# Attention denominators as one run of column-tiled products, other places for the M products, and another order of the first loads

## The chip, the cores and the metric

The kernel runs on one core of a Trainium2 chip. The metric is the device time of one execution in microseconds (us). Executions of one kernel agree within about 0.2%; all runs here are in the fast state (granted TensorE clock 0.997 to 1.0). The experiments ran in several rounds on several chips, each beside the kernel before, whose median moved from 739.8 to 740.2 us between them: differences of some tenths of a us between kernels of different rounds are not resolved by the medians alone.

Engine names in the profile: PE is TensorE's matmuls, PEld its weight loads, DVE is VectorE, ACT is ScalarE, POOL is GpSimd, SP issues the DMAs.

## The reference, cut to what matters

```python
xn = layernorm(x)                                   # x: 2048 x 1024
q, k, v = heads(xn @ wqkv)                          # 32 heads of 32
phi = lambda t: where(t > 0, t + 1, exp(t)) + 1e-6
kv  = einsum("bhsd,bhse->bhde", phi(k), v);  z = phi(k).sum(s)
den = einsum("bhqd,bhd->bhq", phi(q), z) + 1e-6
s   = (phi(q) @ kv / den) @ wo
g   = silu((silu(x_ @ w_gate) * (x_ @ w_up)) @ w_down)   # x_ = xn
out = x + s * g
```

## The kernel before

The kernel works in two passes over 1024 rows each. Within a pass the big products (q, gate, up, then down and the attention output) are split by Strassen's scheme into seven products each, so PSUM banks are scarce: a bank has to be drained by ScalarE or VectorE before TensorE may start the next product in it. `M` is the product of the summed `kv` and `wo`, made of 16 small products in pass 0.

The program is not written in its final order. Every operation is recorded, and a scheduler in Python then runs a simple simulation with a planned duration per operation, and fixes from it the order in which each engine's queue holds its instructions. On the chip each queue is worked off in that order: in the traces of the changed kernel and of a_twice (below), which share a plan, all 1395 VectorE instructions come in the same order although their waits differ. So an instruction that has to wait holds up all that stand behind it.

```python
def mm_cost(mms):                                   # TensorE, us
    return sum(max(r.shape[-1] / 2400.0 + 0.0026, 0.03) for (_, _, r, _, _) in mms)
def act(reads, writes, o, i, func, src="ps", **kw): # ScalarE
    return PL.op("act", reads, writes, lambda h: h.activation(o, i, func, **kw),
                 nel(o) / 1200.0 + (0.055 if src == "ps" else 0.095))
def dve(reads, writes, fn, n, rate=0.96):           # VectorE
    return PL.op("dve", reads, writes, fn, n / (rate * 1000.0) + 0.07)
...                                                 # in Plan.schedule, for every engine but TensorE:
    rdy = [o for o in a if o.ready <= t]
    o = min(rdy, key=lambda o: (o.dl, o.idx)) if rdy else min(a, key=lambda o: (o.ready, o.dl))
    ...
    free[e] = s + o.busy
    o.done = s + o.busy + o.lat
```

The denominators: after each evicted tile of phi(q), a pair of products with 32 output columns each is put off by seven steps; all pairs of a pass collect in one bank. `recip` then evicts, inverts and stores them, and `normalise_part` scales phi(q) later.

```python
def den_mm():
    if p not in den:
        den[p] = (balloc_part(), set())
    db, seen = den[p]
    mms = []
    for q in (2 * j, 2 * j + 1):
        mms.append((ps[db][32 * q:32 * q + 32, 0:256], Zh[:, g, :],
                    o[:, (q % 2) * 256:(q % 2) * 256 + 256], q not in seen, False))
        seen.add(q)
    pe_mm([named("Zh", g), zh_r, orr], [bank_r[db]], mms)
defer(7, den_mm)
```

Of the kernel before, what the change touches and what calls it, by code (L numbers as in the profile page):

```python
# [9 lines left out]
ACT = mybir.ActivationFunctionType  # L10
ALU = mybir.AluOpType
# [6 lines left out]

class Op:
    __slots__ = ("eng", "fn", "busy", "lat", "nbytes", "sem", "preds", "succs", "idx", "dl", "start", "done",  # L20
                 "ev", "pecum", "npred", "ready", "urgent")


class Region:
# [6 lines left out]
class Plan:  # L31
# [14 lines left out]
    def op(self, eng, reads, writes, fn, busy, sem=None, nbytes=0, urgent=0.0, cow=None, after=None):  # L46


        o = Op()
        o.eng, o.fn, o.busy, o.sem, o.nbytes, o.urgent = eng, fn, busy, sem, nbytes, urgent  # L50
        o.lat = 0.0 if sem is not None else self.LAT[eng]
        o.idx = len(self.ops)
        preds = set()
        for r in reads:
            for k in r.keys:
                preds.update(self.lastw.get(k, ()))
        if cow is not None:
            preds.update(cow.preds)
        if after is not None:
            preds.add(after)  # L60
        for r in writes:
            for k in r.keys:
                if cow is None:
                    preds.update(self.lastw.get(k, ()))
                    preds.update(self.readers.get(k, ()))
        for r in reads:
            for k in r.keys:
                self.readers.setdefault(k, []).append(o)
        for r in writes:
            for k in r.keys:  # L70
                if cow is None:
                    self.lastw[k] = [o]
                    self.readers[k] = []
                else:
                    self.lastw[k].append(o)
        o.preds = preds
        o.succs = []
        for p in preds:
            p.succs.append(o)
        o.pecum = self.pecum  # L80
        if eng == "pe":
            self.pecum += busy
            self.lastpe = o
        self.ops.append(o)
        return o

    def schedule(self):
        ops = self.ops
        for o in reversed(ops):
            d = o.pecum if o.eng == "pe" else o.pecum + 30.0  # L90
            for s in o.succs:
                extra = (4.0 + o.nbytes / 200e3) if o.sem is not None else o.busy + o.lat
                d = min(d, s.dl - extra)
            o.dl = d - o.urgent
        pes = [o for o in ops if o.eng == "pe"]
        cum = [o.pecum + o.busy for o in pes]
        for o in ops:
            if o.sem is not None and o.succs:
                k = bisect_right(cum, o.dl - self.lead) - 1
                if k >= 0 and pes[k] not in o.preds:  # L100
                    o.preds.add(pes[k])
                    pes[k].succs.append(o)
        for o in ops:
            o.npred = len(o.preds)
            o.ready = 0.0
        free = {e: 0.0 for e in self.ENGS}
        dma_free = 0.0
        avail = {e: [] for e in self.ENGS}
        pe_next = deque(o for o in ops if o.eng == "pe")
        for o in ops:  # L110
            if o.npred == 0:
                avail[o.eng].append(o)
        order = []
        done = set()
        total = len(ops)
        while len(order) < total:
            best = None
            for e in self.ENGS:
                a = avail[e]
                if not a:  # L120
                    continue
                t = free[e]
                if e == "pe":
                    lim = None
                    n = 0
                    for o in pe_next:
                        if n >= self.window:
                            lim = o.idx
                            break
                        n += 1  # L130
                    cand = [o for o in a if lim is None or o.idx < lim]
                    if not cand:
                        continue
                    rdy = [o for o in cand if o.ready <= t + 0.05]
                    o = min(rdy, key=lambda o: o.idx) if rdy else min(cand, key=lambda o: (o.ready, o.idx))
                else:
                    rdy = [o for o in a if o.ready <= t]
                    o = min(rdy, key=lambda o: (o.dl, o.idx)) if rdy else min(a, key=lambda o: (o.ready, o.dl))
                s = max(t, o.ready)
                if best is None or s < best[0]:  # L140
                    best = (s, e, o)
            s, e, o = best
            o.start = s
            if o.sem is not None:
                free[e] = s + 0.08
                b = max(s + 1.0, dma_free)
                dma_free = b + o.nbytes / 230e3
                o.done = dma_free + 1.8
            else:
                free[e] = s + o.busy  # L150
                o.done = s + o.busy + o.lat
            avail[e].remove(o)
            if e == "pe":
                done.add(o)
                while pe_next and pe_next[0] in done:
                    pe_next.popleft()
            order.append(o)
            for q in o.succs:
                q.npred -= 1
                q.ready = max(q.ready, o.done)  # L160
                if q.npred == 0:
                    avail[q.eng].append(q)
        self.order = order
        return order
# [55 lines left out]
def build_kernel(nc, A_x, A_wqkv, A_wo, B_w_gate, B_w_up, B_w_down, out, WINDOW=6, NWARM=14, NPE=4, LEAD=12.0):  # L220
# [12 lines left out]
    with ExitStack() as es:  # L233
# [20 lines left out]
        def named(*key):  # L254
            return Region([key])
# [30 lines left out]
        banks = deque(range(8))  # L286
        bare = deque()
        is_bare = set()

        def balloc(fresh=False):  # L290

            if fresh and bare:
                b = bare.popleft()
                is_bare.discard(b)
                return b
            return banks.popleft()
# [5 lines left out]
            return b  # L302

        def bfree(b):
            (bare if b in is_bare else banks).append(b)

        def sem(name):
# [350 lines left out]
        def t_tile(i):  # L658
# [10 lines left out]
            for q, halves in enumerate(((0, 4), (4, 4)) if i == 0 else ((0, 8),)):  # L669
# [3 lines left out]
                pe_tr([s.r, ident_r], [bank_r[b]],  # L673
                      [(pb[:, k, :], xa[:, (k0 + k) * 128:(k0 + k + 1) * 128], ident[:, :]) for k in range(n)])
                xr = xt_r(i, k0, n)
                if q == 0:
                    act([bank_r[b]], [xr], dst[:, k0:k0 + n], pb, ACT.Identity)
                else:
                    dve([bank_r[b]], [xr], lambda h, k0=k0, n=n, pb=pb: h.tensor_copy(dst[:, k0:k0 + n], pb), n * 128)
# [113 lines left out]
                st.direct = direct  # L793
            return st

        for n, (fn, args) in enumerate(((x_load, (0,)), (wkv_load, (0, 1, 0)), (x_load, (1,)), (wkv_load, (0, 1, 1)),
                                        (wkv_load, (0, 0, 0)), (wkv_load, (0, 0, 1)), (x_load, (2,)),
                                        (wkv_load, (1, 1, 0)), (wkv_load, (1, 1, 1)), (x_load, (3,)),
                                        (wkv_load, (1, 0, 0)), (wkv_load, (1, 0, 1)))):
# [211 lines left out]
        def q_load(p, s):  # L1011
            return wload(wqkv_v[:, :, s * 512:(s + 1) * 512], QJ[p][s])

        den = {}
        PQ0 = 52 * KB

        def pq_tile(g, j):
# [3 lines left out]
        def q_pair(p, s, stats, at, go=True):  # L1021
            stat, jstat = stats

            def evac(w):
                def f(i, j, ap, r, bank):
                    g = 2 * (2 * s + w) + i
                    o, orr = pq_tile(g, j)
                    phi_evac(ap, r, o, orr, "ps" if bank is not None else "sb")

                    def den_mm():  # L1030
                        if p not in den:
                            den[p] = (balloc_part(), set())
                        db, seen = den[p]
                        mms = []
                        for q in (2 * j, 2 * j + 1):
                            mms.append((ps[db][32 * q:32 * q + 32, 0:256], Zh[:, g, :],
                                        o[:, (q % 2) * 256:(q % 2) * 256 + 256], q not in seen, False))
                            seen.add(q)
                        pe_mm([named("Zh", g), zh_r, orr], [bank_r[db]], mms)
                    defer(7, den_mm)  # L1040
                return f
            s0, s1 = (xset(stat, w, XV[p], evac(w), d_ring) for w in range(2))
            pair = Pair(s0, s1, joint_of(jstat, s0, s1) if QJ[p][s] else None, at)
# [3 lines left out]

        def recip(p):

            flush()  # L1050
            db = den[p][0]
            e = rr_ring.take()
            ea, ra, rb = e.ap(F32, 0, KB), e.ap(F32, KB, KB), e.ap(BF16, 0, KB // 2)
            er, rr = e.sub(0, KB).r, e.sub(KB, KB).r
            dve([bank_r[db]], [er], lambda h: h.tensor_scalar(ea, ps[db][:, 0:256], 16.0, EPS_PHI, ALU.mult, ALU.add), 256)
            bfree(db)
            for q in range(4):
                dve([er], [e.sub(KB + q * 256, 256).r], lambda h, q=q: h.reciprocal(
# [290 lines left out]
        for p in range(2):  # L1349
            for k, n in order:  # L1350
# [2 lines left out]
                if (p, k, n) == (0, "q", 0):  # L1353
                    at = {"5_1": [kv_done], "3_0": [kvt]}
                if p == 0 and (k, n) in (("g", 0), ("q", 1), ("u", 0)):
                    at = {w: [build_m] for w in ("2_1 6_1 7_1 3_1 4_1" + " 2_0" * (k == "u")).split()}
                if (k, n) == ("u", 0):
                    at["7_0"] = at.get("7_0", []) + [partial(recip, p)]
                if n == 1 and k in "gu":
                    at = {w: [partial(normalise_part, p, "gu".index(k), h)] for h, w in enumerate(("2_1", "7_1"))}  # L1360
                if last_pair[0] is not None and (p, k, n) == (1, "q", 0):
                    pass
                elif k == "q":
# [81 lines left out]
```

## Time and profile before

739.85 us, the median of 3 runs (739.5 to 740.21). The profiled execution spans 739.1 us.

| what | number | view |
|---|---|---|
| TensorE busy | 722.5 us | page, part 1 |
| share of the chain of work that ended last: PE, ACT, DVE | 86%, 7%, 4% | page, part 4 |
| start to start of 512- and 256-column matmuls | 216 and 109 ns | timeline |
| time that 2790, 868 and the small ones need at that rate | about 707 us | worked out |
| TensorE's late starts from 125 to 715 us | 7.1 us | timeline, summed |

The two lines of the page that this rests on: busy time by engine, and the chain that ended last, by engine.

```profile
PE 722.5 (98%) x3878; PEld 365.9 (50%) x3894; DVE 599.3 (81%) x1398; ACT 396.6 (54%) x740; POOL 16.2 (2%) x35
PE 86%; ACT 7%; DVE 4%; DMA 1%; issue 1%; SPq 0%; POOL 0%; ACTq 0%
```

TensorE bounds the kernel. As matmuls overlap (a 512-column one is shown 379 ns long, and the next starts 216 ns after it), "busy" hides short losses, so I read starts: the next lines are the timeline of TensorE (start us, us, engine, line, operation, out<-in, form, count, and in brackets idle time and what ended it).

```profile
133.48 0.38 PE L209 MATMUL ps<-W 128*128 128x256 f16 x2
133.70 0.38 PE L209 MATMUL ps<-X,W 128*128 128x256 f16 x2
134.01 0.29 PE L209 MATMUL ps<-H,Zh 128*32 128x256 bf16 x2
134.23 0.39 PE L209 MATMUL ps<-W 128*128 128x256 f16 x2
134.46 0.81 PE L209 MATMUL ps<-X,W 128*128 128x512 f16 x3
...
474.33 0.38 PE L209 MATMUL ps<-TM,X 128*128 128x256 f16 x2
474.64 0.52 PE L209 MATMUL ps<-H,Zh 128*32 128x256 bf16 x8
475.48 0.61 PE L209 MATMUL ps<-X 128*128 128x512 f16 x2 [0.32 <-DVE ps L344]
```

Two 256-column products take 0.22 us from start to start (133.48 to 133.70). Before the denominator pair (`H,Zh`, 128*32) it is 0.31 (133.70 to 134.01) and after it another 0.22. A lone pair thus costs 0.31 us: 93 ns to get in, and 216 ns until the next product starts. At 474.64, four pairs that happen to stand together take 0.23 us from first to last start.

Where TensorE waits for others: these lines of its timeline have the longest brackets between 200 and 715 us, in the normalisation of pass 0 and in the q stage of pass 1.

```profile
211.22 0.39 PE L209 MATMUL ps<-X,W 128*128 128x256 f16 x2 [0.35 <-ACT ps L337]
223.66 0.39 PE L209 MATMUL ps<-X,W 128*128 128x256 f16 x2 [0.50 <-ACT ps L337]
...
441.23 0.39 PE L209 MATMUL ps<-P,W 128*128 128x256 f16 x2 [0.93 <-DVE H L707]
...
449.17 0.60 PE L209 MATMUL ps<-P,W 128*128 128x512 f16 x2 [1.03 <-ACT ps L337]
```

And the table by stretches (length, then busy us and count of PE, PEld, DVE, ACT, POOL, the clock, DMA share and GB/s). VectorE works 110.5 of 114 us in this stretch of pass 1.

```profile
core 0: us, PE busy (x) PEld busy (x) DVE busy (x) ACT busy (x) POOL busy (x), PEclk, DMA share, GB/s
436.00:550.00 114.00, 111.35 (x651) 60.17 (x650) 110.47 (x280) 80.43 (x160) 0.00 (x0) 1.00 0.40 127
```

### The profile page before, as it was taken

How to read it: one execution, taken by the hardware profiler on the slowest of the kernel's cores; microseconds unless marked ns; L12 is line 12 of the kernel's file. 1: busy time of each engine (PE TensorE's matmuls, PEld its weight loads, DVE VectorE, ACT ScalarE, POOL GpSimd, SP SyncE). 2: the span in 40 equal slices, each digit the busy share in tenths (PEclk: the TensorE clock that was granted, in tenths of full speed). 3: DMA queues.
4: the chain of work that ended last, by engine and by line, in shares of the span. 5: the costliest groups of instructions: out<-in, count | busy, mean ns of one | idle time of the engine just before them, and what ended most of it. 6: DMA issues, size and time to landing. Idle time of an engine off the chain costs nothing.

```text
span 739.1 us, 10502 instructions
## 1 busy us (share of the span) xinstructions
PE 722.5 (98%) x3878; PEld 365.9 (50%) x3894; DVE 599.3 (81%) x1398; ACT 396.6 (54%) x740; POOL 16.2 (2%) x35
## 2 busy tenths in 40 slices
PE   7999999999999999999999999999999999999996
PEld 3444444454555555544444444455555555444442
DVE  6989868989899988886466879999998988757353
ACT  2776554787696565623232266577866655223231
POOL 2201100000000000000000000000000000000000
PEclk9999999999999999999999999999999999999999
DMA  9363235124573323371846434217525245374822
GB/s 302 96 114 72 44 109 175 59 79 158 162 243 104 115 62 110 100 232 40 198 113 167 150 106 111 97 62 229 182 103 172 72 136 152 90 164 109 184 65 50
DMA packets 135219, 94.00 MB, mean 127 GB/s; under 512 B 32512, under 2 KB 131072, under 8 KB 135168
## 3 DMA queue, kind: packets, MB, share of 16 engines
q1 hardware_dynamic: 135168, 93.34, 44.5%
q8 instruction: 30, 0.49, 0.3%
q14 instruction: 21, 0.17, 0.1%
HBM read 75.50 MB, written 10.62 MB: 117 GB/s over the span
## 4 chain that ended last, share of the span: by engine, by line
PE 86%; ACT 7%; DVE 4%; DMA 1%; issue 1%; SPq 0%; POOL 0%; ACTq 0%
PE ps L209 86%; ACT TM L337 3%; ACT H L337 3%; DMA W<-in_A_x_dram 1%; ACT L337 1%; DVE H L707 1%; DVE W L344 1%; ACT ps L337 1%; DVE TM L706 0%; ACT W L337 0%; DVE H L344 0%; PE ps L216 0%; DVE TM L344 0%; DVE stats L637 0%; ACT X L337 0%
## 5 line engine op out<-in xcount | busy, mean ns | idle before, releaser
L209 PE MATMUL ps<-X,W 128*128 128x512 f16 (+1 forms) x1408 | 312.9, 361 | 1.1 <-ACT ps L337 0.9
L337 ACT ACTIVATE TM<-ps 128x512 f16<-128x512 f32 (+2 forms) x337 | 182.0, 557 | 156.6 <-PE ps L209 154.0
L209 PE MATMUL ps<-H,W 128*128 128x512 f16 (+1 forms) x891 | 206.1, 379 | 0.9 <-DVE TM L707 0.4
L209 PEld LDWEIGHTS ps<-X,W 128*128 128x128 f16 (+1 forms) x1408 | 136.1, 98 | 120.5 <-ACT ps L337 1.4
L344 DVE TENSOR_TENSOR W<-W 128x256 f16<-128x256 f16 (+6 forms) x424 | 170.0, 440 | 7.8 <-DMA W<-in_B_w_down_dram 5.7
L344 DVE TENSOR_TENSOR ps<-ps,TM 128x256 f32<-128x256 f32 (+1 forms) x218 | 117.5, 540 | 34.1 <-PE ps L209 33.1
L209 PEld LDWEIGHTS ps<-H,W 128*128 128x128 f16 (+1 forms) x896 | 87.1, 98 | 104.2 <-DVE TM L707 0.9
L337 ACT ACTIVATE H<-ps 128x512 f16<-128x512 f32 (+1 forms) x126 | 75.3, 602 | 64.6 <-PE ps L209 64.4
L337 ACT ACTIVATE ps<-ps 128x512 f32<-128x512 f32 (+1 forms) x156 | 78.7, 505 | 57.6 <-PE ps L209 52.6
L209 PE MATMUL ps<-P,W 128*128 128x256 f16 (+1 forms) x440 | 90.0, 323 | 2.1 <-ACT ps L337 1.0
L209 PE MATMUL ps<-W 128*128 128x256 f16 (+1 forms) x328 | 70.3, 299 | 0.5 <-DVE W L344 0.3
L344 DVE TENSOR_TENSOR TM<-ps,TM 128x512 f32<-128x512 f32 (+1 forms) x60 | 40.9, 682 | 31.2 <-PE ps L209 30.9
L337 ACT ACTIVATE TM<-TM 128x512 f16<-128x512 f32 (+1 forms) x61 | 38.0, 622 | 48.9 <-DVE TM L344 47.4
L209 PEld LDWEIGHTS ps<-P,W 128*128 128x128 f16 (+1 forms) x440 | 42.5, 98 | 34.1 <-ACT ps L337 1.7
L344 DVE TENSOR_TENSOR H<-H,TM 128x512 f16<-128x512 f16 x112 | 45.8, 417 | 12.9 <-ACT H L337 12.5
L344 DVE TENSOR_TENSOR H<-H 128x1024 f16<-128x1024 f16 (+2 forms) x82 | 50.3, 629 | 0.8 <-PE ps L209 0.3
L209 PEld LDWEIGHTS ps<-W 128*128 128x128 f16 (+1 forms) x328 | 30.9, 98 | 27.1 <-DVE W L344 2.7
L344 DVE TENSOR_TENSOR TM<-TM 128x512 f16<-128x512 f16 (+1 forms) x59 | 24.2, 419 | 18.6 <-DMA TM<-TM 11.0
L209 PE MATMUL ps<-H,X 128*128 128x512 bf16 (+1 forms) x133 | 32.5, 380 | 2.5 <-ACT X L337 0.7
L344 DVE TENSOR_TENSOR W<-H 128x1024 f16<-128x1024 f16 x40 | 26.9, 685 | 5.2 <-PE ps L209 4.9
L209 PE MATMUL ps<-TM,W 128*128 128x256 f16 (+1 forms) x144 | 30.9, 296 | 0.0
L706 DVE TENSOR_SCALAR TM<-TM 128x512 f16<-128x512 f16 x64 | 18.0, 286 | 10.6 <-ACT TM L337 10.5
(82 smaller groups left out, 419.4 us busy)
## 6 DMA issues: line engine op xcount, KB each, us to landing
W<-in_B_w_gate_dram SPq DMA_DIRECT2D x14, 1024.0 KB, 5.2
W<-in_B_w_up_dram SPq DMA_DIRECT2D x14, 1024.0 KB, 5.2
W<-in_B_w_down_dram SPq DMA_DIRECT2D x16, 896.0 KB, 6.2
W<-in_A_x_dram SPq DMA_DIRECT2D x16, 256.0 KB, 3.1
H<-in_A_wqkv_dram SPq DMA_DIRECT2D x8, 512.0 KB, 8.5
W<-in_A_wqkv_dram SPq DMA_DIRECT2D x4, 1024.0 KB, 5.3
H<-r_scratch SPq DMA_DIRECT2D x32, 128.0 KB, 3.8
q_scratch<-H SPq DMA_DIRECT2D x8, 512.0 KB, 3.1
```

The costliest lines, as they stand in the source:

```text
L209: last = h.matmul(o, l, r, start=st, stop=sp, skip_group_check=True)
L337: return PL.op("act", reads, writes, lambda h: h.activation(o, i, func, **kw), nel(o) / 1200.0 + (0.055 if src == "ps" else 0.095))
L344: return dve(reads, writes, lambda h: h.tensor_tensor(o, a, b, op), nel(o), 1.92 if fast else 0.96)
L706: dve([e.r], [b.r], lambda h: h.tensor_scalar(ba, ea, 1.0, EPS_PHI, ALU.min, ALU.add), 512, 2.6)
L707: dve([src_r, b.r], [out_r], lambda h: h.scalar_tensor_tensor(out_ap, src, 0.0, ba, ALU.max, ALU.add), 512)
```

## The change

Its intent: spend the change of tiling mode once a pass, not at each pair; hold no bank for the denominators during the q products; put the M products where banks are free; and load the first two tiles of x before the weights.

```diff
@@ balloc: which bank a fresh product gets
-            if fresh and bare:
+            if fresh and bare and (len(banks) < 3 or freed[bare[0]] < freed[banks[0]]):
@@ transposes of the first tile
-                if q == 0:
+                if q == 0 or i == 0:
                     act([bank_r[b]], [xr], dst[:, k0:k0 + n], pb, ACT.Identity)
@@ first loads
-        ... ((x_load, (0,)), (wkv_load, (0, 1, 0)), (x_load, (1,)), (wkv_load, (0, 1, 1)),
+        ... ((x_load, (0,)), (x_load, (1,)), (wkv_load, (0, 1, 0)), (wkv_load, (0, 1, 1)),
@@ den_mm is gone; recip
-            flush()
-            db = den[p][0]
+            db = balloc_part()
+            mms, rd = [], [zh_r]
+            for g in range(NG):
+                rd.append(named("Zh", g))
+                for q in range(4):
+                    o, orr = pq_tile(g, q // 2)
+                    rd.append(orr)
+                    mms.append((ps[db][32 * q:32 * q + 32, 0:256], Zh[:, g, :],
+                                o[:, (q % 2) * 256:(q % 2) * 256 + 256], g == 0, False))
+            pe_mm(rd, [bank_r[db]], mms)
...
-            dve([bank_r[db]], [er], lambda h: h.tensor_scalar(ea, ps[db][:, 0:256], 16.0, EPS_PHI, ...), 256)
+            act([bank_r[db], eps_r], [er], ea, ps[db][:, 0:256], ACT.Identity, bias=epsc[:, :], scale=16.0)
@@ where the steps stand (k: q, gate or up; n: block)
-                    at = {w: [build_m] for w in ("2_1 6_1 7_1 3_1 4_1" + " 2_0" * (k == "u")).split()}
-                if (k, n) == ("u", 0):
-                    at["7_0"] = at.get("7_0", []) + [partial(recip, p)]
-                if n == 1 and k in "gu":
-                    at = {w: [partial(normalise_part, p, "gu".index(k), h)] for h, w in enumerate(("2_1", "7_1"))}
+                    at = {"2_0": [build_m], "6_0": [build_m], "2_1": [build_m] * 2, "6_1": [build_m] * 2}
+                if (k, n) == ("g", 1):
+                    at = {"2_1": [partial(recip, p)]}
+                if (k, n) in (("u", 1), ("g", 2)):
+                    at = {w: [partial(normalise_part, p, "ug".index(k), h)] for h, w in enumerate(("2_1", "7_1"))}
```

Some lines of the change (a field `boost`, always 0) have no effect and are left out.

More of the change, by code (lines that the diff above doesn't have):

```diff
@@ L20 @@
     __slots__ = ("eng", "fn", "busy", "lat", "nbytes", "sem", "preds", "succs", "idx", "dl", "start", "done",
-                 "ev", "pecum", "npred", "ready", "urgent")
+                 "ev", "pecum", "npred", "ready", "urgent", "boost")
 class Region:
@@ L51, in op @@
         o.lat = 0.0 if sem is not None else self.LAT[eng]
+        o.boost = 0.0
         o.idx = len(self.ops)
@@ L137, in schedule @@
                     rdy = [o for o in a if o.ready <= t]
-                    o = min(rdy, key=lambda o: (o.dl, o.idx)) if rdy else min(a, key=lambda o: (o.ready, o.dl))
+                    o = min(rdy, key=lambda o: (o.dl - o.boost, o.idx)) if rdy else min(a, key=lambda o: (o.ready, o.dl))
                 s = max(t, o.ready)
@@ L288, in build_kernel @@
         is_bare = set()
+        freed = [0] * 8
         def balloc(fresh=False):
-            if fresh and bare:
+            if fresh and bare and (len(banks) < 3 or freed[bare[0]] < freed[banks[0]]):
                 b = bare.popleft()
@@ L304, in bfree @@
         def bfree(b):
+            freed[b] = len(PL.ops)
             (bare if b in is_bare else banks).append(b)
@@ L794, in kv_set @@
             return st
-        for n, (fn, args) in enumerate(((x_load, (0,)), (wkv_load, (0, 1, 0)), (x_load, (1,)), (wkv_load, (0, 1, 1)),
+        for n, (fn, args) in enumerate(((x_load, (0,)), (x_load, (1,)), (wkv_load, (0, 1, 0)), (wkv_load, (0, 1, 1)),
                                         (wkv_load, (0, 0, 0)), (wkv_load, (0, 0, 1)), (x_load, (2,)),
@@ L1012, in q_load @@
             return wload(wqkv_v[:, :, s * 512:(s + 1) * 512], QJ[p][s])
-        den = {}
         PQ0 = 52 * KB
@@ L1028, in f @@
                     phi_evac(ap, r, o, orr, "ps" if bank is not None else "sb")
-                    def den_mm():
-                        if p not in den:
-                            den[p] = (balloc_part(), set())
-                        db, seen = den[p]
-                        mms = []
-                        for q in (2 * j, 2 * j + 1):
-                            mms.append((ps[db][32 * q:32 * q + 32, 0:256], Zh[:, g, :],
-                                        o[:, (q % 2) * 256:(q % 2) * 256 + 256], q not in seen, False))
-                            seen.add(q)
-                        pe_mm([named("Zh", g), zh_r, orr], [bank_r[db]], mms)
-                    defer(7, den_mm)
                 return f
@@ L1054, in recip @@
             er, rr = e.sub(0, KB).r, e.sub(KB, KB).r
-            dve([bank_r[db]], [er], lambda h: h.tensor_scalar(ea, ps[db][:, 0:256], 16.0, EPS_PHI, ALU.mult, ALU.add), 256)
+            act([bank_r[db], eps_r], [er], ea, ps[db][:, 0:256], ACT.Identity, bias=epsc[:, :], scale=16.0)
             bfree(db)
```

## The prediction

> **What bounds the kernel now.** TensorE. The page has PE busy 722.5 of 739.1 us at full clock, and PE with 86% of the chain of work that ended last. In the timeline, 512-column matmuls start every 216 ns and 256-column ones every 109 ns; the program's 2790 and 868 of these, with the small ones, need about 707 us. The rest is start-up, tail, waits and the denominator products.
>
> **Denominators (the main term).** In the timeline each pair of 32-column products starts 309 ns after a 512-column matmul instead of 216 (93 ns, the length of their weight load), its two products start 3 ns apart, and what follows starts 216 ns later. So a lone pair costs 0.31 us of PE. Pass 0 has 16 lone pairs (5.0 us); pass 1 has 12 entries, some of several pairs (about 4 us). The trace already shows short runs: at 474.6 us four pairs follow each other at 115 and 106 ns, and four products start within 5 ns. This agrees with the Trainium skill, "TensorEngine Tiling (Array Packing)", Key Properties: a change of tiling mode drains the engine, different tiles run in parallel. A run of 32 is then 8 groups of four at 0.11 us plus one entry and one exit: an estimate of 1.1 us a pass. Saved: 9.0 - 2.2 = 6.8 us of PE work.
>
> **Waits around it.** Starts later than these rates allow, summed from the timeline: about 1.6 us at 139-163 us (M products waiting for a bank that ScalarE drains), 1.2 us at 211 and 224 us (ScalarE full: 9.5 of 10 and 11.9 of 12 us, normalisation), 2.9 us at 437, 441, 449 and 475 us. The den bank is no longer held through the q pairs and M products move to steps with more free banks; but the new order has four M products in a row, with one bank twice. I expect 1.2 us less in sum. The normalisation moves by one pair with the same ScalarE work, so its waits move rather than vanish.
>
> **What takes some back.** VectorE: the table by stretches has it busy 113 of 116 us from 436 to 550 us, and 39 of 40 from 200 to 240. With PE faster by 4 us in the first of these, VectorE ends some waits. I take off 1.5 us.
>
> **Start.** PE loses 5.2 us in the first 20 us. x tile 1 landed at 7.54 us and should now land near 4.3; but VectorE now does tile 1's statistics before it normalises tile 0, so the first real matmul should come about 1 us later (8.7 instead of 7.65), after which tile 1 no longer interrupts. The later wkv landings (9.1 to 19.4 us) stay, and VectorE is 98% busy from 20 to 40 us. I expect 1.0 us gained.
>
> **Sum.** -6.8 - 1.2 + 1.5 - 1.0 = -7.5 us: 732.3 us, range 729 to 736.5. Faster by over 2%: 0.02; within 2%: 0.97; slower: 0.01.
>
> **What would show it.** 32 products within about 1.0 us, two entries in all. PE's missing time in 128-180 us down by over 4 us, in 436-480 us by 3 to 5. First real matmul near 8.7 us; at 26 us PE about 1 us ahead. From 240 to 420 and 560 to 720 us the rhythm unchanged, only shifted.
>
> **What would make it wrong.** Weight loads of the run not hidden: 0.2 us per group of four, 0.8 us more a pass. VectorE saturated in pass 1, so nothing of that pass's 3 us arrives. M products in a row waiting for ScalarE. A slower start, as both halves of tile 0 now go through ScalarE. Better: all waits near 440-475 us gone, 3 us more.

## The result, and the profile after

735.4 us, the median of 4 runs (735.19 to 735.52), against 740.03 for the kernel before in the same rounds (739.5 to 740.36): 4.6 us less. Ratio 0.9938, 95% interval 0.9921 to 0.9955. Here and below, a ratio is the mean time of one kernel's fast runs over that of the other's of the same rounds, so not quite the ratio of the medians quoted. All outputs are right.

The same two lines of the page after the change:

```profile
PE 717.2 (98%) x3894; PEld 365.8 (50%) x3894; DVE 596.9 (81%) x1395; ACT 397.1 (54%) x743; POOL 14.1 (2%) x35
PE 80%; DVE 11%; ACT 7%; issue 1%; DMA 0%; POOL 0%; ACTq 0%; DVEq 0%
```

TensorE lost 5.3 us of busy time, but its share of the chain fell from 86 to 80%, and VectorE's rose from 4 to 11%. The timeline of TensorE around the run of pass 1 shows both the gain and a new loss:

```profile
478.31 1.03 PE L210 MATMUL ps<-P,W 128*128 128x512 f16 x4
479.26 1.06 PE L210 MATMUL ps<-H,Zh 128*32 128x256 bf16 x32
480.25 1.90 PE L210 MATMUL ps<-X,W 128*128 128x512 f16 x8
481.99 1.46 PE L210 MATMUL ps<-P,W 128*128 128x256 f16 x8
484.54 1.04 PE L210 MATMUL ps<-X,W 128*128 128x512 f16 x4 [1.09 <-DVE ps L347]
...
488.08 0.39 PE L210 MATMUL ps<-W 128*128 128x256 f16 x2 [0.77 <-DVE ps L347]
```

The 32 products take 1.06 us, and the run as a whole delays the next product by 1.08 us, in both passes. But 4 us later TensorE waits 1.09 us and then 0.77 us for VectorE to evict a bank (`ps`). The same stretch in the table shows VectorE as busy as before:

```profile
436.00:550.00 114.00, 110.40 (x664) 61.29 (x663) 110.31 (x283) 81.56 (x162) 0.00 (x0) 1.00 0.41 127
```

An account of the time from the end of the k and v stage (the last product into the `kv` banks) to the end of the program, from the starts of TensorE in the two traces: 617.7 us before, 613.3 after, 4.4 less. The denominators cost 9.1 us before and 2.2 after (-6.9). The late starts of all other products grew by 2.6 us. So the main term came as predicted, and more than a third of it came back as waits. The question of the experiments is why.

### The profile page after: what moved, and what is told of

Same layout as the page of the kernel before. It is cut to its first block, busy times and chain, and to the rows that moved or that the text cites. A ratio compares the mean times of both kernels' runs of the same rounds, so it can differ in the third digit from the quotient of the medians.

```text
span 733.8 us, 10527 instructions
## 1 busy us (share of the span) xinstructions
PE 717.2 (98%) x3894; PEld 365.8 (50%) x3894; DVE 596.9 (81%) x1395; ACT 397.1 (54%) x743; POOL 14.1 (2%) x35
## 4 chain that ended last, share of the span: by engine, by line
PE 80%; DVE 11%; ACT 7%; issue 1%; DMA 0%; POOL 0%; ACTq 0%; DVEq 0%
PE ps L210 79%; DVE W L347 3%; ACT TM L340 3%; ACT H L340 2%; DVE ps L347 2%; DVE H L347 2%; DVE TM L347 1%; DVE H L710 1%; ACT L340 1%; ACT ps L340 1%; DVE stats L640 1%; DVE TM L709 1%; DVE stats L641 0%; DMA W<-in_A_x_dram 0%; POOL rstd L644 0%
```

## The experiments

Two theories stand against each other for the waits that came back:

- **Saturation** (what the prediction said): VectorE is full from 436 to 550 us, so whatever TensorE saves, VectorE's work takes back.
- **Queue order**: VectorE could have evicted in time, but its queue, fixed by the scheduler, holds less urgent work first. The scheduler counts each of the 32 products at 0.109 us, so it planned 3.5 us for a run that takes 1.06.

VectorE's timeline after the run shows what stood before the eviction that TensorE waits for (`ps<-ps,TM` at 483.79):

```profile
480.33 0.67 DVE L347 TENSOR_TENSOR W<-W 128x1024 f16<-128x1024 bf16 x1
480.93 1.41 DVE L347 TENSOR_TENSOR H<-H,TM 128x512 f16<-128x512 f16 x4
482.27 1.40 DVE L347 TENSOR_TENSOR H<-H 128x1024 f16<-128x1024 f16 x2
483.59 0.28 DVE L347 TENSOR_TENSOR W<-W 128x256 f16<-128x256 bf16 x1
483.79 0.69 DVE L347 TENSOR_TENSOR ps<-ps,TM 128x512 f32<-128x512 f32 x1
```

`H<-H` are sums for the down product, which starts at 617 us; `W<-W` are sums of later weights. They can wait.

### b_start: the start alone

Before, with these edits only:

```diff
-  ((x_load, (0,)), (wkv_load, (0, 1, 0)), (x_load, (1,)), ...
+  ((x_load, (0,)), (x_load, (1,)), (wkv_load, (0, 1, 0)), ...
-  if q == 0:
+  if q == 0 or i == 0:
```

> The kernel before with only the start of the change (two x tiles first, both halves of tile 0's transposes evicted by ScalarE). If the parts add up as the two traces suggest, TensorE reaches the denominator of pass 0 0.9 us earlier and the total is 0.9 us shorter (-0.1%). Rival: the gain at the start is lost again in the q stage because VectorE is full there; then the total moves by less than 0.3 us.

740.0 us against 739.94 (ratio 1.0004, 0.9989 to 1.0019). No gain in the timed runs, although its profiled execution spans 0.9 us less than the one of before. The profiled execution of before was a late one: 739.1 us, while those of the same kernel in these rounds span 737.6 to 738.9. See a_tab_nostart for the rest.

### b_den: the run alone

Before, with the run of 32, ScalarE's eviction and the later places of `recip` and `normalise_part` (the diff's parts on these), nothing else.

> The kernel before with only the denominators as one run of 32 (and its later normalisation). Main theory: 7.0 us of TensorE time goes, and 2 to 3 us come back as waits of TensorE for VectorE and ScalarE: -4 to -5 us. Rival: the waits that came back belong to the M products and the new bank rule, not to the run; then this kernel gains 6.5 to 7.5 us and beats the whole change.

736.59 us (ratio 0.9953, 0.9939 to 0.9968): -3.3 us, less than the 4 to 5 expected. The two waits after the run of pass 1 are there as in the whole change (1.09 and 0.77 us idle). These two waits came with the run (and what moved with it), not with the M products or the bank rule.

### b_mprod: the M products and the bank rule alone

```diff
-  at = {w: [build_m] for w in ("2_1 6_1 7_1 3_1 4_1" + ...
+  at = {"2_0": [build_m], "6_0": [build_m], "2_1": [build_m] * 2, "6_1": [build_m] * 2}
-  if fresh and bare:
+  if fresh and bare and (len(banks) < 3 or freed[bare[0]] < freed[banks[0]]):
```

> The kernel before with only the new places of the M products and the new rule by which banks are picked. Main theory: no gain, between +1.0 and -0.3 us, as M products in a row wait for ScalarE (the change showed one wait of 1.4 us there). Rival (the intent of the change): waits of 1.6 us at 139 to 163 us vanish: -1 to -1.6 us.

739.21 us (ratio 0.9988, 0.9973 to 1.0003): between no gain and 2 us; not settled by the times. In its trace about 1.1 us are lost near 154 us, at an M product (its own record is missing), after a table load of ScalarE. What the one trace of each kernel says of its worth stands with the account below.

### a_cost: the run counted right

```diff
-  return sum(max(r.shape[-1] / 2400.0 + 0.0026, 0.03) for (_, _, r, _, _) in mms)
+  return sum(0.03 if o.shape[0] == 32 else max(r.shape[-1] / 2400.0 + 0.0026, 0.03) for (o, _, r, _, _) in mms)
```

No instruction is added or removed; only the order of the queues differs. Compared in the two traces, 68 of VectorE's 1395 places hold another instruction, 8 of ScalarE's 743, and 32 of TensorE's 3894 weight loads.

> The changed kernel, with the run of 32 counted by the kernel's own scheduler as 0.96 us in place of 3.6 (it took 1.06 us by the trace). Queue-order theory: the 1.25 and 0.93 us waits for VectorE just after the run of pass 1 come from the static order of VectorE's queue, made for a run of 3.6 us; they shrink by at least 1.2 us together and the total falls by 1 to 2.5 us. Saturation theory: VectorE has no room there whatever the order; the total moves by less than 0.5 us.

732.43 us (ratio 0.9896, 0.9879 to 0.9913), 3 us below the changed kernel, more than the 1 to 2.5 expected. TensorE and VectorE at the same place as above:

```profile
478.40 1.06 PE L210 MATMUL ps<-H,Zh 128*32 128x256 bf16 x32
479.38 1.90 PE L210 MATMUL ps<-X,W 128*128 128x512 f16 x8
481.12 1.46 PE L210 MATMUL ps<-P,W 128*128 128x256 f16 x8
482.42 1.03 PE L210 MATMUL ps<-X,W 128*128 128x512 f16 x4
483.29 0.60 PE L210 MATMUL ps<-P,W 128*128 128x256 f16 x4
```

```profile
479.70 1.10 DVE L348 TENSOR_TENSOR H<-H,TM 128x512 f16<-128x512 f16 x3
480.71 0.71 DVE L348 TENSOR_TENSOR ps<-ps,TM 128x512 f32<-128x512 f32 x1
481.31 0.43 DVE L348 TENSOR_TENSOR H<-H,TM 128x512 f16<-128x512 f16 x1
```

The eviction stands five places earlier in VectorE's queue; it starts 2.3 us after the run's start instead of 4.5, and no product waits. TensorE's own order near here differs only from 488.08 us on, after the first of the two waits. VectorE does the same work: 596.1 us in the whole program, 596.9 before this edit. Saturation falls as the reason for these waits. They make 2.2 of the 3 us; the other 0.8 us are late starts just after the run of pass 0 (182 to 184 us in the changed kernel), which went too.

### a_twice and a_cost_twice: each denominator product done twice

The run has 64 products and the scale is halved, so the result stays right; the planned duration is kept, so each queue's order is that of the parent (after, or a_cost).

```diff
-  for g in range(NG):
+  for n, g in enumerate(list(range(NG)) * 2):
-  pe_mm(rd, [bank_r[db]], mms)
+  PL.op("pe", rd, [bank_r[db]], partial(_mm_group, mms), mm_cost(mms[:32]))
-  bias=epsc[:, :], scale=16.0)
+  bias=epsc[:, :], scale=8.0)
```

> The changed kernel with each denominator product done twice (64 in a run, scale halved, result right), every engine's order kept. By the trace the 32 more products take 0.88 us a pass of TensorE. Queue-order theory: the scheduler planned 3.6 us for the run, so a longer run only fills the waits after it (2.2 us in pass 1, 0.7 us in pass 0): the total rises by 0 to 0.4 us, and the waits after the run in pass 1 fall from 2.2 to about 1.3 us. If TensorE time counts fully, the total rises by 1.8 us.

> The kernel with the corrected cost of the run, with each denominator product done twice, every engine's order kept. No wait follows the run there, so TensorE time counts fully: +1.5 to +1.8 us against that kernel (both theories), about 734.0 us. Beside the doubled run in the changed kernel this tells whether the same added work is free where waits follow it. If it also rises by under 0.5 us here, TensorE is not what bounds this stage and the queue-order theory falls.

a_twice took 735.24 us (ratio 0.9939, 0.9924 to 0.9954), no more than the changed kernel's 735.4; a_cost_twice took 733.94 (0.9922, 0.9907 to 0.9937), 1.5 more than a_cost. In the traces, from the end of the k and v stage on, a_twice takes as long as its parent (613.3 us both) and a_cost_twice 1.7 us longer (612.0 against 610.3). The added work is the same, 0.87 us a pass: the run's delay goes from 1.08 to 1.96 us in both. In a_twice it only fills the wait behind it, which shrinks from 1.09 to 0.22 us:

```profile
478.84 1.93 PE L210 MATMUL ps<-H,Zh 128*32 128x256 bf16 x64
480.70 1.90 PE L210 MATMUL ps<-X,W 128*128 128x512 f16 x8
482.44 1.46 PE L210 MATMUL ps<-P,W 128*128 128x256 f16 x8
484.12 1.04 PE L210 MATMUL ps<-X,W 128*128 128x512 f16 x4 [0.22 <-DVE ps L347]
```

So in the changed kernel the products after the run were bound by VectorE's queue, and TensorE's time there was free up to the length of that wait; with the right order TensorE bounds again.

### b_den_cost: the run alone, counted right

b_den with the edit of a_cost.

> The kernel before with only the run of 32, counted right by the scheduler. If the run is what the change is worth, and its wrong count what hid it: 3 us below the same kernel with the wrong count, that is 733.5 us, -6.4 us against before; the rest of the change (start, M products, bank rule) is then worth about 1 us. If it stays within 1 us of 736.6 us, the count only mattered together with the other parts.

734.47 us (ratio 0.9926, 0.9911 to 0.9941): -5.3 us against before, where -6.4 was expected and b_den had -3.3. Counting the run right is worth 2.1 us here (3 expected), and its waits of pass 1 are gone. The rest of the change, for which about 1 us was expected, brings 2.0 us beside the counted run (734.47 against a_cost's 732.43). In b_den_cost's trace the M products of pass 0 still cost waits: 1.65 us lost at 138.9 and 1.01 us at 154.7.

### a_tab: table loads counted

ScalarE loads a function table at the start, and again whenever it goes from Exp to Silu or back: ten loads in the program. The scheduler did not know this. The changed kernel's ScalarE and TensorE near the M products (`ps<-H`):

```profile
136.82 1.28 ACT L340 ACT_TABLE_LOAD   x1
138.12 0.60 ACT L340 ACTIVATE TM<-ps 128x512 f16<-128x512 f32 x1
```

```profile
137.12 0.38 PE L210 MATMUL ps<-H 128*128 128x512 bf16 x1
138.77 0.88 PE L210 MATMUL ps<-H 128*128 128x512 bf16 x3 [1.27 <-ACT TM L340]
```

The Trainium skill, "ScalarE: Activation LUTs", section What ACT_TABLE_LOAD costs, gives 1283 ns for the load; all ten in this trace take 1283 ns. The edit, on top of a_cost, without the lines that note the table of each operation:

```diff
+  if o.tab is not None:                       # Exp or Silu; Identity needs no table
+      s += 1.28 if tab not in (None, o.tab) else 0.0
+      tab = o.tab
   free[e] = s + o.busy
```

> The corrected kernel, whose scheduler now also counts 1.28 us for each activation table load of ScalarE (Exp to Silu and back), which it left out; the trace shows one just before the 1.4 us wait of the four M products for a bank. Theory of wrong durations: that wait falls by 0.7 us or more and the total by 0.5 to 1.5 us. Rival (four M products in a row wait for ScalarE however it is planned): less than 0.3 us.

730.11 us (ratio 0.987, 0.9853 to 0.9886), 2.3 below a_cost, more than the 0.5 to 1.5 expected. But the wait that I had named fell by only 0.2 us (1.06 us idle at 138.63). What went are four late starts between 432 and 468 us, in the q stage of pass 1, where four of the ten loads stand (from 427 to 453 us): late starts of the pass fell from 3.7 to 1.9 us. For the wait of the M products, the rival holds so far.

### a_tab_mold: the M products back in their old places

> The kernel with both durations mended (run of 32, table loads) with the M products put back to the places that the kernel before had (one at a step). If three M products next to each other take the banks while ScalarE loads a table, the 1.2 us wait near 138.6 us goes and the total falls by 0.5 to 1.2 us against 730.1. If the new places are worth something by themselves, the total rises by 0.3 us or more.

730.48 us (ratio 0.987, 0.9856 to 0.9885), 0.4 above a_tab, but in other rounds, and the ratios to before are the same: the times do not tell them apart. From the end of the k and v stage on, its trace takes 608.6 us against 608.1. The wait did not go: it moved to the next q product (0.86 us idle at 137.74, until VectorE had evicted a bank). Neither prediction fits well; in the mended kernel the places of the M products are worth at most some tenths of a us. The wait of 134 to 139 us did not hang on which of the two products came next.

### a_tab_zr: the scaling counted right

Normalisation scales 128x512 tiles in SBUF by a per-partition factor. The plan says 0.52 us; five in a row took 3.19 us in the trace of before. The same page (section What ACT_TABLE_LOAD costs, at its end) has about 280 ns + 0.833 ns an element for an activation with one pointer operand, with about 93 ns of overlap between neighbours. An estimate from it for 512 elements is 0.71 us, and 0.61 for one in a row: the trace agrees, with 0.72 us alone and 0.61 from start to start in a row.

The edit, cut to the duration:

```diff
-  nel(o) / 1200.0 + (0.055 if src == "ps" else 0.095)
+  nel(o) / 1200.0 + {"ps": 0.055, "sb": 0.095, "scaled": 0.193}[src]    # scaled: SBUF source with a scale tile
```

> The mended kernel with a third duration mended: ScalarE's scaling of a 128x512 tile in SBUF, planned as 0.52 us, takes 0.62 us when they follow each other in the trace of before. Theory of wrong durations: the waits for ScalarE in the normalisation (0.39 us near 218 us, 1.05 us from 517 to 520 us) shrink by 0.3 us or more in sum. Rival: ScalarE has simply too much work there, and the total moves by less than 0.3 us.

728.54 us (ratio 0.9842, 0.9826 to 0.9858), 1.6 below a_tab. In a_tab TensorE still waited here:

```profile
516.74 0.39 PE L214 MATMUL ps<-P,W 128*128 128x256 f16 x2 [0.50 <-ACT ps L345]
```

In a_tab_zr no wait is left in either normalisation. This is the fastest kernel, below both the kernel before and the changed one. Its chain that ended last, and the stretch of pass 1:

```profile
PE 95%; DVE 3%; ACT 1%; issue 1%; POOL 0%; DVEq 0%; ACTq 0%; POOLq 0%
```

```profile
436.00:550.00 114.00, 113.69 (x685) 64.08 (x684) 113.13 (x288) 82.80 (x165) 0.00 (x0) 1.00 0.45 141
```

VectorE is busy 113.1 of 114 us, more than ever, and TensorE hardly waits for it. (As the kernel is faster, the stretch holds more work: 685 matmuls, against 664 in the changed kernel.)

### a_tab_nostart: the old start in the mended kernel

> The mended kernel with the start of the kernel before (tile 1 of x third in the queue, second half of tile 0 by VectorE). The profiled trace of before was one with a late start (span 739.1, others of it 737.6 to 738.9), so the 0.9 us read from it may be chance: then this run is within 0.4 us of 730.1. If the start is worth what the prediction said, it is at 731.1.

730.03 us, the median of 4 runs (ratio 0.9862, 0.9847 to 0.9877), against 730.11 with the new start. The new start is worth nothing that these times show. It may make the start more alike: in the traces the k and v stage ends at 120.0 to 120.5 us in the eight kernels with the new start, and at 119.7 to 121.7 in the six with the old one. The times do not show this: the four of a_tab all span 728.4 us and those here 727.8 to 728.6, but those of b_start, with the new start, 738.2 to 739.6.

### b_dur: the kernel before with all durations mended

The edits of a_tab and a_tab_zr in the kernel before, and 0.155 us for each 32-column product (0.31 for a pair, as traced). Its work is that of before.

> The kernel before, unchanged but for the scheduler's durations, all mended: 0.31 us for a pair of denominator products, 1.28 us for a table load, 0.62 us for the scaling of a tile. Its waits of 4.3 us that the mended kernels lost (211, 224, 441, 449, 475, 516 us) should go in part: -2 to -4 us, 736 to 738 us. Then the change itself is worth, with right durations in both, 7.5 to 9.5 us (728.5 against this run), more than the 4.6 us seen. If instead this run comes near 732 us, most of what the experiments won had nothing to do with the change; if it stays at 740, the mended durations help only because of the change.

735.94 us (ratio 0.9943, 0.9926 to 0.996): -4.1 us, just past the range expected and nearly as much as the 4.6 us of the whole change. With right durations on both sides the change is worth 735.9 - 728.5 = 7.4 us, about what its denominators save.

### The account

| kernel | median us | ratio to before | from the end of k and v on, us | late starts, 125 to 715 us |
|---|---|---|---|---|
| before | 739.8 to 740.2 | 1 | 617.7 | 7.1 |
| the change | 735.4 | 0.9938 | 613.3 | 9.7 |
| + run counted right (a_cost) | 732.43 | 0.9896 | 610.3 | 6.7 |
| + table loads (a_tab) | 730.11 | 0.987 | 608.1 | 4.7 |
| + scaling (a_tab_zr) | 728.54 | 0.9842 | 606.6 | 3.2 |
| before, durations mended (b_dur) | 735.94 | 0.9943 | 613.3 | about 2.9 |

The fourth column is read from one trace each and leaves the start out. Kernels that differ in the start alone agree there to 0.1 us (before and b_start: 617.7 and 617.8; a_tab and a_tab_nostart: 608.1 both), so it tells smaller differences apart than the medians do. By it, the M products' places and the bank rule together bring 0.9 us alone (b_mprod: 616.8), 1.1 us beside the run (b_den's 614.5 against 613.3) and 1.9 us beside the run counted right (b_den_cost's 612.2 against 610.3). In the last case the late starts from 128 to 180 us are 4.4 against 2.5 us.

The last column is the sum over TensorE's products of how much later each starts than its predecessor's rhythm allows, from one trace each (places where a record is missing taken out); the trace's own entry and exit of the denominators are not in it.

## Why the prediction was right or wrong

The measured 735.4 us lies inside the stated range (729 to 736.5), and 4.6 us were gained where 7.5 were forecast. By its parts:

- **Denominators, right.** Predicted: 9.0 us of TensorE time become 2.2. Measured: 9.1 become 2.2. The run took 1.06 us with the weight loads hidden, and the estimate came from the short runs that the trace of before already showed. This also agrees with the Trainium skill as cited there, that a change of mode drains the engine and that tiles run in parallel: here the entry costs 93 ns once, and four products start within 10 ns.
- **Waits around it, wrong in sign.** "I expect 1.2 us less in sum", with 1.5 us taken back by VectorE: +0.3 together. Measured +2.6. By place, in late starts: +0.9 us from 128 to 180 us, +0.8 after the run of pass 0, -0.9 in the normalisation of pass 0, -0.9 in the q stage of pass 1, +2.1 after the run of pass 1, +0.7 in the normalisation of pass 1. So the prediction's own test, over 4 us less missing from 128 to 180 us, failed: it is about 3.0 us (6.6 become 3.6). The M products in a row did wait (1.27 us), as feared. The normalisation's waits did not just move; they fell from 1.3 to 0.4 us in pass 0 (0.33 and 0.07 us of late start at 219.5 and 219.8) and grew from 0.4 to 1.1 us in pass 1.
- **What takes some back: a wrong reason.** The step "VectorE ends some waits" because it is busy 113 of 116 us (110.5 of 114 in the table above) was read from a busy share. The waits were there (1.09 and 0.77 us), but a_cost removed them with the same VectorE work, and the best kernel has VectorE busier still. What failed is the order in its queue. I had read the diff and the order of instructions, but not compared the durations that the scheduler assumes with the trace; that the plan for the run was 3.5 us against 1.1 predicted could have been seen before any run.
- **Start, wrong.** "I expect 1.0 us gained." The first real matmul came at 8.72 us, as predicted (8.7), and tile 1 landed at 4.37, but the gain was not there in the times of b_start and a_tab_nostart. The 7.54 us at which tile 1 landed in the trace of before was no fixed cost: the same loads, in the same order, landed it anywhere from 5.76 to 7.99 us in five other traces (a_tab_nostart, b_den, b_mprod, b_den_cost, b_dur).
- **Rhythm elsewhere, right.** From the first down product of pass 0 to the first q product of pass 1 both traces take 95.3 us, and from the first down product of pass 1 to the end both take 116.5.
- **The total, partly luck.** One of the four terms of the sum came true. The measured time lies 1.1 us from the slow end of the range, inside it because the range was wide enough for the waits and the start to be misjudged by 2.9 us in all.

What stays open: how much of the gain is due to the bank that the denominators no longer hold, which no run separates from the run itself; what the M products' places and the bank rule are worth one by one (together about 0.9 to 1.9 us by the traces; b_mprod's times alone, within 2 us, do not resolve it); and the 1.9 to 2.7 us of late starts from 133 to 140 us that no variant with the run lost. In b_dur, where TensorE is slower in that stage, nearly all of them are absent, which fits ScalarE and VectorE being too slow there for a faster TensorE; this is argued, not shown.

## What to carry to other kernels

Where a static scheduler orders in-order queues, a change to one operation's real duration is also a change to the plan: put the durations that the trace shows into its cost function together with the change, and the fixed overheads (table loads, operand setup) too. Here that was worth 4.1 us in the kernel before and 6.9 in the changed one, against 4.6 for the change itself. Before blaming a full engine for a wait, look at what stood in its queue before the awaited instruction, and whether that could have come later. And compare a start-up gain with several traces, as the same first load landed up to 2.2 us apart here (5.76 to 7.99 us, six traces).

## What the Trainium skill lacked or had wrong

- "ScalarE: Activation LUTs", What ACT_TABLE_LOAD costs: it adds a drain of about 1380 ns to each switch. Here the last activation before the load ends at 136.80 us, and the next starts at 138.12: 1.31 us in all, as at eight of the nine switches of this trace; no drain seen.
- "TensorE: Matmul & The Clock Gate", Back-to-back issue gap: it gives 131 ns for each 512-column matmul in a stream with weight loads. Here such a stream, each matmul with its own load, starts every 216 ns, which is what the page has for the isolated gap.
- The same page, section The mechanism, "What overlaps and what doesn't": weight loads are said to overlap matmuls in flight only in other row groups. Here, with all 128 rows in use, the loads of 128x128 weights (98 ns) are hidden in the 216 ns rhythm, and those of 128x32 weights (92 to 97 ns) between groups of four products of the same column tiles that start about 111 ns apart. (Under Step-by-step the same page also allows loads into a background weight buffer, which would fit.)
- "TensorEngine Tiling (Array Packing)", Key Properties: it has no figure for the change of mode. Here it is 93 ns on entry, and 205 to 216 ns from the last tiled start to the next full one.
- "Perfetto Trace Analysis", Identifying the Most-Contended Engine: it says to optimise the engine of highest occupancy first. From 436 to 550 us VectorE's went from 110.3 in the changed kernel to 113.1 of 114 us in a_tab_zr, while the waits for it all but went away; occupancy alone did not tell that the order of its queue was at fault.
- No page that I found has the spread of a first load's landing: 5.76 to 7.99 us for the same load in the same place of the queue, in six executions.
